# Sliding-window attention on TensorE: token tiles of 128 rows by 32 columns, or of 64 rows by 32 columns with even and odd tokens apart

## The chip, the cores and the metric

The kernel runs on one core of a Trainium2 chip. The metric is the device time of one execution in microseconds (us), the median over several runs. TensorE (PE in the profile, PEld for its weight loads) multiplies matrices and writes its results to PSUM. VectorE (DVE) and ScalarE (ACT) work element by element. SyncE (SP) issues the transfers (DMA) and works through them in order.

## What is computed

x has 2048 tokens of 1024 features, in bf16. Two mixers alternate, each applied twice:

```python
def _A_ref(x, wqkv, wo):              # H = 32 heads, Dh = 32
    W, dil = 8, 2
    qkv = (lambda x, *d: x.transpose(*d))((x @ wqkv).reshape(B, S, 3, H, Dh), 2, 0, 3, 1, 4)
    q, k, v = qkv[0], qkv[1], qkv[2]
    idx = pos[:, None] - (jnp.arange(W) * dil)[None, :]        # 8 keys: token s, s-2, ..., s-14
    ...
    logits = jnp.where(mask, jnp.einsum("bhsd,bhswd->bhsw", q, kg) * scale, -1e9)
    o = jnp.einsum("bhsw,bhswd->bhsd", _softmax(logits, axis=-1), vg)
    return o.transpose(0, 2, 1, 3).reshape(B, S, D) @ wo

def _B_ref(x, w1, b1, w2, b2):        # F = 3584, over the tokens
    u = _gelu(jnp.einsum("bsd,sf->bdf", _layernorm(x), w1) + b1)
    return (jnp.einsum("bdf,fs->bds", u, w2) + b2).transpose(0, 2, 1)

for _ in range(2):
    x = x + _A_ref(_layernorm(x), A_wqkv, A_wo)
    x = x + _B_ref(_layernorm(x), B_w1, B_b1, B_w2, B_b2)
```

A token attends to itself and to seven earlier ones at distances 2, 4, ..., 14: even tokens see only even ones, odd tokens only odd ones.

## The kernel before

The two classes of tokens are called c = 0 and 1. Class c has 1024 tokens, in NI = 8 tiles (c, i) of 128 tokens. Before the change a tile holds tokens of one class only, so that eight neighbours of the window are eight adjacent columns. The 32 heads lie in NG = 8 groups g of four.

One layer runs in stages. The first layer begins with `start_up`: tiles of x are loaded (`x_load`, line 218), normalised on VectorE, transposed into hT by transposing transfers (`T_`, line 281) and multiplied by the value weights (`V_`, line 269); its four queues PE, ACT, DVE and SP are written out by hand, and each engine follows its own list in order. The second layer has hT from the end of `gemm2` and computes the values in `v_proj`.

The attention follows. A unit u is one group of heads and one class; a visit is half a unit, four tiles of 128 tokens, so a layer has 32 visits. In each visit, in this order on TensorE:

- `scores(u, b)` (line 408): keys are the weights, 32 columns at a time; the moving operand is the query qB, which holds each head's query in its own 32 rows and zeros in the others, four heads of 40 columns, 160 in all. ScalarE takes the exponential (line 411) into pc, and `mask` (line 423) on VectorE multiplies by the band into the persistent buffer Pm, in four instructions, one for each 32 partitions.
- `values` of the visit before: value weights of 32 columns against Pm (line 443; line 439 is the overlap from the block before), and the sums of the weights by a matrix of ones (lines 447 and 456). The results lie in the two banks of one PSUM tile, acc, of which there is one buffer. ScalarE makes the reciprocal with a logarithm and an exponential (lines 459, 460), and VectorE multiplies it in (line 462, called norm here), into oT.
- two `qk_chunk`s (line 377): eight matmuls of 512 columns each, the queries or keys of a later unit, in m tiles, of which there are two. ScalarE copies them out (lines 384, 381). The query goes to its rows in qB by VectorE copies (line 388) or by transfers (line 390).

`in_order` keeps TensorE to this written order, and `chain_` keeps another engine to the order in which it is called. In the last two visits of a layer the output projection (`out_proj`, line 492, with its residual add, line 499, and its statistics, line 510) takes the place of the `qk_chunk`s, and there VectorE's order is chained, with the mask in two parts around an add. Then come the rest of the output projection, `gemm1` (line 572) and `gemm2` (line 619), which are dense 128x128 matmuls.

Of the kernel before, what the change touches and what calls it, by code (L numbers as in the profile page):

```python
# [14 lines left out]
P = 128  # L15
# [10 lines left out]
def kernel(  # L26
# [33 lines left out]
    KW = P + W  # L60
    KG = 32
    GW = KG + W
    HB = NI // 2
# [89 lines left out]
    qB = [pers.tile([P, HG, SC + W], BF16, name=f"qB{n}") for n in range(2)]  # L153
    kT = [pers.tile([P, SC], BF16, name=f"kT{n}") for n in range(2)]
    Pm = pers.tile([P, HG, NS * HB, KW], BF16, name="Pm")

    def zero_fill():
        nc.vector.memset(Pm[:].rearrange("p h t k -> p (h t k)"), 0.0)
        for t in qB:
            r = nc.vector.memset(t[:].rearrange("p h t -> p (h t)"), 0.0)  # L160
        return r
# [5 lines left out]
    out_v = out2d.rearrange("(i p c) d -> c i p d", p=P, c=DIL)  # L167
    wq_v = A_wqkv.rearrange("(kt p) c -> p kt c", p=P)
# [32 lines left out]

    last = {}
# [5 lines left out]
    def start_up(v, wv):  # L208
# [3 lines left out]
        def x_load(k, hs=(slice(0, D),)):  # L212
            c, i = order[k]
# [3 lines left out]
            for h in hs:  # L217
                r = nc.sync.dma_start(out=xs[k][:, h], in_=xin_v[c, i][:, h])
# [42 lines left out]
        def C_(k, hf):  # L261
            ks = slice(hf * KD // 2, (hf + 1) * KD // 2)
            return nc.scalar.copy(out=hT[:, ks, cols(*order[k])], in_=tps[k, hf][:])

        def V_(k, n, kts):
            if k not in pss_:
                pss_[k] = a_tile() if k % 3 == 1 else s_tile()
            for kt in kts:
                r = nc.tensor.matmul(pss_[k][:, n, :], lhsT=hT[:, kt, cols(*order[k])], rhs=wv[kt // 2][:, kt % 2, n * 512:(n + 1) * 512],  # L269
# [3 lines left out]
        def E_(k):  # L273
            c, i = order[k]
            dst, src = v[c][i][:].rearrange("p (n d) -> p n d", n=NDC), pss_[k][:]
# [4 lines left out]
        def T_(k):  # L280
            return nc.sync.dma_start_transpose(out=hT[:, :, cols(*order[k])], in_=xs[k])
# [76 lines left out]
    def v_proj(v, c, i, wv, ns):  # L358
        for n in ns:
            ps = m_tile()  # L360
            for kt in range(KD):
                nc.tensor.matmul(ps[:], lhsT=hT[:, kt, cols(c, i)], rhs=wv[kt // 2][:, kt % 2, n * 512:(n + 1) * 512],  # L362
                                 start=(kt == 0), stop=(kt == KD - 1))
            nc.scalar.copy(out=v[c][i][:, n * 512:(n + 1) * 512], in_=ps[:])
# [7 lines left out]
    def qk_chunk(u, wts, part, n):  # L372
        g, c = divmod(u, DIL)
        ps = m_tile()
        lo = c * SC + n * 512
        for kt in range(KD):
            mm = nc.tensor.matmul(ps[:], lhsT=wts[part][:, kt, (g % 2) * P:(g % 2 + 1) * P], rhs=hT[:, kt, lo:lo + 512],  # L377
                                  start=(kt == 0), stop=(kt == KD - 1))
        ls = slice(n * 512, (n + 1) * 512)
        if part:  # L380
            nc.scalar.copy(out=kT[u % 2][:, ls], in_=ps[:])  # L381
        else:
            qs = gop.tile([P, 512], BF16, name="qs", tag="go")
            nc.scalar.copy(out=qs[:], in_=ps[:])  # L384
            for h in range(HG):
                hp = slice(h * DH, (h + 1) * DH)
                if h < 1 + 2 * n or u == 0:
                    nc.vector.tensor_copy(out=qB[u % 2][hp, h, ls], in_=qs[hp, :])  # L388
                else:
                    chain_("SP", lambda: nc.sync.dma_start(out=qB[u % 2][hp, h, ls], in_=qs[hp, :]))  # L390
# [8 lines left out]
    def scores(u, b):  # L399
        q, k = qB[u % 2], kT[u % 2]  # L400
        s0 = (2 * u + b) % NS * HB
        ss = s_tile()
        for i in range(HB):
            lo = (b * HB + i) * P
            for r in range(P // KG):
                rp = slice(r * KG, (r + 1) * KG)
                dst = ss[rp, i // 2, i % 2 * HG * GW:(i % 2 + 1) * HG * GW].rearrange("p (h k) -> p h k", k=GW)
                mm = nc.tensor.matmul(dst, lhsT=k[:, lo + r * KG:lo + (r + 1) * KG],  # L408
                                      rhs=q[:, :, lo + r * KG:lo + r * KG + GW], start=True, stop=True)
        pc = pcp.tile([P, HB, HG, GW], BF16, name="pc", tag="pc")  # L410
        nc.scalar.activation(out=pc[:].rearrange("p (n t) h k -> p n (t h k)", n=2), in_=ss[:, :, 0:2 * HG * GW],  # L411
# [344 lines left out]
```

## Time and profile before

| | |
|---|---|
| time, three runs | 1290.9, 1290.99 and 1291.12 us; median 1290.99 |
| span of the profiled execution | 1288.8 us (its own time is not given; the median is 2.2 us more) |
| TensorE busy | 1273.3 us, 99% of the span |
| VectorE, ScalarE busy | 417.6 us (32%), 368.9 us (29%) |
| granted TensorE clock | 1.000 |
| attention of the first layer, 69.6 to 203 us | TensorE 130.3, VectorE 93.7, ScalarE 89.3 us busy |
| matmuls of lines 408, 443, 447 in all | 29.5 us, 36.9 us, 24.8 us busy |

The span runs from the first to the last instruction. A matmul's duration in the rows holds its way through the array, so neighbouring matmuls overlap in the rows; the distance of their starts tells what each costs. "issue" as a reason for idle time means that nothing which the profile shows was waited for; here it stands where the array changes between tiles of 128x128 and of 128x32. A tile is named in the views by its name in the program.

### The profile page before, as it was taken

How to read it: one execution, taken by the hardware profiler on the slowest of the kernel's cores; microseconds unless marked ns; L12 is line 12 of the kernel's file. 1: busy time of each engine (PE TensorE's matmuls, PEld its weight loads, DVE VectorE, ACT ScalarE, POOL GpSimd, SP SyncE). 2: the span in 40 equal slices, each digit the busy share in tenths (PEclk: the TensorE clock that was granted, in tenths of full speed). 3: DMA queues.
4: the chain of work that ended last, by engine and by line, in shares of the span. 5: the costliest groups of instructions: out<-in, count | busy, mean ns of one | idle time of the engine just before them, and what ended most of it. 6: DMA issues, size and time to landing. Idle time of an engine off the chain costs nothing.

```text
span 1288.8 us, 19376 instructions
## 1 busy us (share of the span) xinstructions
PE 1273.3 (99%) x8266; PEld 591.8 (46%) x8422; DVE 417.6 (32%) x855; ACT 368.9 (29%) x609; POOL 2.4 (0%) x15
## 2 busy tenths in 40 slices
PE   9999999999999999999999999999999999999999
PEld 4444444444444444444444444444444444444444
DVE  7467777820000022322300677688000000111111
ACT  4366664431111110000033666645311111000000
POOL 0000000000000000000000000000000000000000
PEclk9999999999999999999999999999999999999999
DMA  8711124652232244564500111247323222334321
GB/s 239 113 47 50 48 83 134 199 148 73 66 90 68 58 129 121 138 166 124 137 27 1 50 48 51 80 153 222 110 69 94 68 63 83 98 106 138 116 92 33
DMA packets 204103, 126.59 MB, mean 98 GB/s; under 512 B 44273, under 2 KB 183793, under 8 KB 204017
## 3 DMA queue, kind: packets, MB, share of 16 engines
q1 hardware_dynamic: 204016, 125.35, 34.4%
q8 instruction: 66, 1.08, 0.4%
q14 instruction: 21, 0.16, 0.0%
HBM read 96.48 MB, written 16.78 MB: 88 GB/s over the span
## 4 chain that ended last, share of the span: by engine, by line
PE 98%; issue 1%; DMA 0%; DVE 0%; ACT 0%
PE m L377 17%; PE s L619 15%; PE s L572 15%; PE m L492 9%; PE acc L572 7%; PE m L572 7%; PE acc L619 7%; PE m L619 7%; PE m L362 4%; PE s L269 3%; PE s L408 2%; PE acc L269 1%; PE acc L443 1%; PE acc L447 1%; DMA x<-in_A_x_dram 0%
## 5 line engine op out<-in xcount | busy, mean ns | idle before, releaser
L619 PEld LDWEIGHTS <-w 128*128 128x128 bf16 x1820 | 177.0, 98 | 210.2
L572 PEld LDWEIGHTS <-w 128*128 128x128 bf16 x1792 | 175.4, 98 | 211.4
L377 PE MATMUL m<-hT,wqk 128*128 128x512 bf16 x962 | 223.5, 379 | 6.2 <-issue 4.4
L572 PE MATMUL s<-h,w 128*128 128x512 bf16 x878 | 201.3, 379 | 0.8
L619 PE MATMUL s<-g,w 128*128 128x512 bf16 (+1 forms) x912 | 201.0, 374 | 0.7
L621 DVE SCALAR_TENSOR_TENSOR xo<-s,b_sb,xs 128x512 bf16<-128x512 f32 (+1 forms) x33 | 24.4, 739 | 532.9 <-PE s L619 526.6
L377 PEld LDWEIGHTS <-wqk 128*128 128x128 bf16 x1024 | 95.2, 98 | 118.0 <-issue 10.7
L423 DVE TENSOR_TENSOR Pm<-pc,band 32x640 bf16<-32x640 bf16 x256 | 123.6, 483 | 56.2 <-ACT pc L411 49.4
L492 PE MATMUL m<-wo,oT 128*128 128x512 bf16 x500 | 110.6, 379 | 0.8 <-issue 0.3
L572 PE MATMUL acc<-h,w 128*128 128x512 bf16 x440 | 103.1, 379 | 0.5
L619 PE MATMUL acc<-g,w 128*128 128x512 bf16 x436 | 99.7, 379 | 0.5
L572 PE MATMUL m<-h,w 128*128 128x512 bf16 x438 | 98.4, 379 | 0.5
L619 PE MATMUL m<-g,w 128*128 128x512 bf16 (+1 forms) x436 | 96.9, 376 | 0.6
L178 ACT ACTIVATE ln<-mv,eps 128x1 f32<-128x1 f32 x64 | 18.9, 295 | 231.4 <-DVE mv L186 184.8
L492 PEld LDWEIGHTS <-oT 128*128 128x128 bf16 x512 | 49.6, 98 | 60.4 <-issue 1.3
L579 ACT ACTIVATE g<-s,b_sb 128x1024 bf16<-128x1024 f32 x28 | 31.2, 1114 | 158.2 <-PE s L572 146.4
L388 DVE COPY qB<-qs 32x512 bf16<-32x512 bf16 x136 | 38.2, 281 | 95.5 <-ACT qs L384 94.2
L362 PE MATMUL m<-wv,hT 128*128 128x512 bf16 x251 | 55.2, 379 | 0.3
L411 ACT ACTIVATE pc<-s,shift 128x640 bf16<-128x640 f32 x64 | 51.2, 800 | 11.7 <-PE s L408 11.7
L384 ACT CAST qs<-m 128x512 bf16<-128x512 f32 x64 | 37.5, 586 | 48.3 <-PE m L377 47.2
L381 ACT CAST kT<-m 128x512 bf16<-128x512 f32 x64 | 37.5, 586 | 46.4 <-PE m L377 46.4
L499 DVE TENSOR_TENSOR xn<-m,xr 128x512 bf16<-128x512 f32 x64 | 44.2, 691 | 16.9 <-PE m L492 16.4
(67 smaller groups left out, 678.9 us busy)
## 6 DMA issues: line engine op xcount, KB each, us to landing
w<-in_B_w_dram SPq DMA_DIRECT2D x56, 512.0 KB, 3.7
w<-in_B_w_dram SPq DMA_DIRECT2D x64, 448.0 KB, 4.4
wqk<-in_A_wqkv_dram SPq DMA_DIRECT2D x16, 512.0 KB, 5.0
xa<-xn SPq DMA_DIRECT2D x32, 256.0 KB, 2.2
xs<-xa SPq DMA_DIRECT2D x32, 256.0 KB, 3.1
wo<-in_A_wo_dram SPq DMA_DIRECT2D x8, 512.0 KB, 5.3
xr<-in_A_x_dram SPq DMA_DIRECT2D x16, 256.0 KB, 3.3
xb<-xo SPq DMA_DIRECT2D x16, 256.0 KB, 2.6
```

What stands on the lines that cost most here:

```text
L269: r = nc.tensor.matmul(pss_[k][:, n, :], lhsT=hT[:, kt, cols(*order[k])], rhs=wv[kt // 2][:, kt % 2, n * 512:(n + 1) * 512], start=(kt == ...
L362: nc.tensor.matmul(ps[:], lhsT=hT[:, kt, cols(c, i)], rhs=wv[kt // 2][:, kt % 2, n * 512:(n + 1) * 512], start=(kt == 0), stop=(kt == KD - 1))
L377: mm = nc.tensor.matmul(ps[:], lhsT=wts[part][:, kt, (g % 2) * P:(g % 2 + 1) * P], rhs=hT[:, kt, lo:lo + 512], start=(kt == 0), stop=(kt = ...
L381: nc.scalar.copy(out=kT[u % 2][:, ls], in_=ps[:])
L384: nc.scalar.copy(out=qs[:], in_=ps[:])
L388: nc.vector.tensor_copy(out=qB[u % 2][hp, h, ls], in_=qs[hp, :])
L411: nc.scalar.activation(out=pc[:].rearrange("p (n t) h k -> p n (t h k)", n=2), in_=ss[:, :, 0:2 * HG * GW], func=ACT.Exp, scale=scale, bia ...
L423: mm = nc.vector.tensor_tensor(out=Pm[rp, :, s0:s0 + HB, r * KG:r * KG + GW].rearrange("p h t k -> p t h k"), in0=pc[rp], in1=mk, op=ALU.mult)
L492: mm = nc.tensor.matmul(ps[:], lhsT=oT[g][:, cols(c, i)], rhs=wo[n][g // 4][:, g % 4, :], start=(g == 0), stop=(g == NG - 1))
L499: return nc.vector.tensor_tensor(out=xn[:, xs_], in0=pss_["o", n][:], in1=xr[:, xs_], op=ALU.add)
L572: nc.tensor.matmul(pairs[fl][0][dc], lhsT=wt[c][:, i, fl * P:(fl + 1) * P], rhs=h2[c][i][:, dc * 512:(dc + 1) * 512], start=(k == 0), stop ...
L619: nc.tensor.matmul(ap, lhsT=w2t[ft // HF][:, ft % HF, c::DIL], rhs=g[ft // GF][:, ft % GF, lo:lo + w], start=(ft == 0), stop=(ft == FT - 1))
```

## The change

A tile t now holds 128 consecutive tokens, the 64 even ones in rows 0 to 63 and the 64 odd ones in rows 64 to 127. `hT`, `v` and `kT` follow this order; `qB` keeps two slots instead of four, since two heads share 64 rows. A visit is four such tiles of one group of heads (512 tokens, both classes).

- `scores` makes one matmul for 32 keys and two heads (64 rows, 80 columns) where there was one for four heads (128 rows, 160 columns). The head pairs e = 0 and 1 write different PSUM banks.
- `values` makes one matmul for each class (64 rows, 72 columns instead of 136) and likewise for the sums (256 columns instead of 512); class c has PSUM bank c of acc, the values in its first half and the sums in its second.
- the query and key projections run two and three chunks ahead; each query chunk has two VectorE copies and two transfers.
- each tile of x is loaded by two transfers (the first tile by four), and in `gemm2` of the first layer each tile is transposed by two transfers.
- the output projection takes its tiles in another order (four at a time from both classes) and in half tiles: one in visit 29, two each in visits 30 and 31, the others after. VectorE's order is chained in these three visits, with the mask in one piece.

The functions' lines before stand in the listing above; of `qk_chunk`, `scores`, `values` and the visits' loop the lines after are shown.

```diff
-    KW = P + W
     KG = 32
     GW = KG + W
-    HB = NI // 2
+    KH = P // DIL
+    KW = KH + W
+    HB = 4
+    NQ = NT // HB
+    QC = HB * KH
+    NV = NG * NQ
...
-    qB = [pers.tile([P, HG, SC + W], BF16, name=f"qB{n}") for n in range(2)]
-    kT = [pers.tile([P, SC], BF16, name=f"kT{n}") for n in range(2)]
+    qB = [pers.tile([P, 2, DIL, SC + W], BF16, name=f"qB{n}") for n in range(2)]
+    kT = [pers.tile([P, S], BF16, name=f"kT{n}") for n in range(2)]
     Pm = pers.tile([P, HG, NS * HB, KW], BF16, name="Pm")
...
+    xin_m = x_in.rearrange("(t m c) d -> t c m d", m=KH, c=DIL)
...
             if k % 2 == 0:
                 x_load.t = gop.tile([P, GF, D], BF16, name="x0", tag="go")
             xs[k] = x_load.t[:, k % 2, :]
             for h in hs:
-                r = nc.sync.dma_start(out=xs[k][:, h], in_=xin_v[c, i][:, h])
+                for c in range(DIL):
+                    r = nc.sync.dma_start(out=xs[k][half(c), h], in_=xin_m[k, c][:, h])
...
+    def qk_chunk(part, k, wts):
+        g, n = divmod(k, NQ)
         ps = m_tile()
+        lo = n * 512
         for kt in range(KD):
+            mm = nc.tensor.matmul(ps[:], lhsT=wts[g // 2][part][:, kt, (g % 2) * P:(g % 2 + 1) * P],
+                                  rhs=hT[:, kt, lo:lo + 512], start=(kt == 0), stop=(kt == KD - 1))
         if part:
+            nc.scalar.copy(out=kT[g % 2][:, lo:lo + 512], in_=ps[:])
         else:
+            qs = gop.tile([P, DIL, QC], BF16, name="qs", tag="go")
+            nc.scalar.copy(out=qs[:].rearrange("p c (t m) -> p t c m", m=KH),
+                           in_=ps[:].rearrange("p (t c m) -> p t c m", c=DIL, m=KH))
             for h in range(HG):
                 hp = slice(h * DH, (h + 1) * DH)
+                dst = qB[g % 2][hp, h % 2, :, n * QC:(n + 1) * QC]
+                if h % 2 == 0 or k < 2:
+                    nc.vector.tensor_copy(out=dst, in_=qs[hp])
                 else:
+                    chain_("SP", lambda: nc.sync.dma_start(out=dst, in_=qs[hp]))
...
+    def scores(vis):
+        g, b = divmod(vis, NQ)
+        q, k = qB[g % 2], kT[g % 2]
         ss = s_tile()
         for i in range(HB):
+            t = b * HB + i
             for r in range(P // KG):
+                c, f = divmod(r, KH // KG)
                 rp = slice(r * KG, (r + 1) * KG)
+                lo = t * KH + f * KG
+                for e in range(2):
+                    ep = slice(e * 2 * DH, (e + 1) * 2 * DH)
+                    dst = ss[rp, e, i * 2 * GW:(i + 1) * 2 * GW].rearrange("p (h k) -> p h k", k=GW)
+                    mm = nc.tensor.matmul(dst, lhsT=k[ep, t * P + r * KG:t * P + (r + 1) * KG],
+                                          rhs=q[ep, :, c, lo:lo + GW], start=True, stop=True)
         pc = pcp.tile([P, HB, HG, GW], BF16, name="pc", tag="pc")
+        nc.scalar.activation(out=pc[:].rearrange("p t (e h) k -> p e t (h k)", e=2),
+                             in_=ss[:, :, 0:2 * HB * GW].rearrange("p e (t x) -> p e t x", t=HB),
                              func=ACT.Exp, scale=scale, bias=shift[:])
+        exps[:] = pc, vis % NS * HB
...
+            lo = r % (KH // KG) * KG
+            mm = nc.vector.tensor_tensor(out=Pm[rp, :, s0:s0 + HB, lo:lo + GW].rearrange("p h t k -> p t h k"),
...
+    def values(vis, v, oT):
+        g, b = divmod(vis, NQ)
         acc = a_tile()
         t0 = b * HB
+        s0 = vis % NS * HB
         sp = (s0 - 1) % (NS * HB)
+        hc = [(h, c) for h in range(HG) for c in range(DIL)]
         for i in range(-1 if b else 0, HB):
+            for h, c in hc:
+                hp, cp = slice(h * DH, (h + 1) * DH), half(c)
+                lhs = v[t0 + i][cp, g * P + h * DH:g * P + (h + 1) * DH]
                 if i < 0:
+                    dst, src = acc[hp, c, 0:W], Pm[cp, h, sp, KH:KW]
                 else:
+                    w = KW if i < HB - 1 else KH
+                    dst, src = acc[hp, c, i * KH:i * KH + w], Pm[cp, h, s0 + i, 0:w]
+                nc.tensor.matmul(dst, lhsT=lhs, rhs=src, start=(i == (-1 if b else 0)), stop=False, skip_group_check=True)
         runs = [(s0, HB - 1, 1)]
         if b:
             runs = [(sp, HB, 0)] if sp < s0 else [(sp, 1, 0)] + runs
+        for lo_, n_, t_ in [(s0, HB, None)] + runs:
+            for h, c in hc:
+                hp, cp = slice(h * DH, (h + 1) * DH), half(c)
+                dst = acc[hp, c, QC:2 * QC].rearrange("p (t q) -> p t q", q=KH)
+                if t_ is None:
+                    src = Pm[cp, h, lo_:lo_ + n_, 0:KH]
+                else:
+                    dst, src = dst[:, t_:t_ + n_, 0:W], Pm[cp, h, lo_:lo_ + n_, KH:KW]
+                mm = nc.tensor.matmul(dst, lhsT=ones[cp], rhs=src, start=False, stop=t_ is not None, skip_group_check=True)
+        rd = x2("rd", [P, DIL, QC], FP32)
+        nc.scalar.activation(out=rd[:], in_=acc[:, :, QC:2 * QC], func=ACT.Ln)
         nc.scalar.activation(out=rd[:], in_=rd[:], func=ACT.Exp, scale=-1.0)
+        dst = oT[g][:].rearrange("p (c s) -> p c s", c=DIL)[:, :, b * QC:(b + 1) * QC]
+        norm.append(lambda: nc.vector.tensor_tensor(out=dst, in0=acc[:, :, 0:QC], in1=rd[:], op=ALU.mult))
...
-    order = [(c, i) for c in range(DIL) for i in range(NI)]
+    order = [(c, i) for b in range(NQ) for c in range(DIL) for i in (2 * b, 2 * b + 1)]
...
-            nc.sync.dma_start_transpose(out=hT[:, :, cols(c, i)], in_=xs[:])
-
-    NU = NG * DIL
+            for e in range(2):
+                lo = (2 * i + e) * P + c * KH
+                nc.sync.dma_start_transpose(out=hT[:, :, lo:lo + KH], in_=xs[half(e)])
...
+        def half_tile():
+            if not cur:
+                cur.extend(out_proj(*next(tiles), oT, wo, res, xa[li], h2))
+                n = 0
+            else:
+                n = 1
+            in_order(cur[0], n)
+            chain_("DVE", cur[1], n)
+            if n:
+                cur[2]()
+                lns.append(list(cur[3]))
+                cur.clear()
+
+        for part, k in ((0, 0), (0, 1), (1, 0), (0, 2), (1, 1)):
+            in_order(qk_chunk, part, k, wts)
+        for vis in range(NV):
+            ends = vis >= NV - 3
+            if vis % (2 * NQ) == 2 and vis // (2 * NQ) + 1 < NG // 2:
+                nx = vis // (2 * NQ) + 1
+                wts[nx] = [None, None]
+                chain_("SP", load_qk, nx, wts[nx])
+            if vis == NV - 8:
                 wo = []
                 chain_("SP", load_wo, wo)
+            if vis == NV - 3:
                 todo[:] = order
                 for _ in range(3):
                     load_xr(res)
+            in_order(scores, vis)
+            if ends:
+                chain_("DVE", mask, 0, 1, 2, 3)
+            else:
                 mask(0, 1, 2, 3)
             if vis:
+                in_order(values, vis - 1, v, oT)
+                if ends:
+                    chain_("DVE", norm.pop())
+                else:
                     norm.pop()()
+            for part, k in ((0, vis + 3), (1, vis + 2)):
+                if k < NV:
+                    in_order(qk_chunk, part, k, wts)
+                elif ends:
+                    half_tile()
                     ln_step()
+        in_order(values, NV - 1, v, oT)
+        n = 0
+        for n in range(2 * NT - 5):
+            if n in (17, 21):
+                chain_("SP", load_w1, (n - 17) // 4)
+            half_tile()
+            ln_step()
+            if norm:
+                chain_("DVE", norm.pop())
```

## The prediction

> **What bounds the kernel now.** I read the page first: the engines' shares and the chain that ended last.
>
> ```profile
> span 1288.8 us, 19376 instructions
> PE 1273.3 (99%) x8266; PEld 591.8 (46%) x8422; DVE 417.6 (32%) x855; ACT 368.9 (29%) x609; POOL 2.4 (0%) x15
> ...
> PE 98%; issue 1%; DMA 0%; DVE 0%; ACT 0%
> ```
>
> TensorE (PE) is the path nearly everywhere, so only its time counts, and whatever makes it wait. The change touches the attention stages (some 133 us in each layer by the stage windows) and their two ends. So I read TensorE's timeline over two visits (start, duration, engine, line, tile, count):
>
> ```profile
> 117.93 0.46 PE L408 MATMUL s<-qB,kT 128*32 128x160 bf16 x16
> 118.22 0.41 PE L443 MATMUL acc<-Pm,v 128*32 128x136 bf16 x16
> 118.45 0.39 PE L447 MATMUL acc<-Pm,ones 128*32 128x512 bf16 x4
> 118.67 0.18 PE L456 MATMUL acc<-Pm,ones 128*32 128x24 bf16 x4
> 118.78 3.63 PE L377 MATMUL m<-hT,wqk 128*128 128x512 bf16 x15
> 122.34 0.46 PE L408 MATMUL s<-qB,kT 128*32 128x160 bf16 x16
> 122.63 0.18 PE L439 MATMUL acc<-Pm,v 128*32 128x8 bf16 x4
> 122.66 0.40 PE L443 MATMUL acc<-Pm,v 128*32 128x136 bf16 x16
> ...
> 126.78 0.46 PE L408 MATMUL s<-qB,kT 128*32 128x160 bf16 x16
> ```
>
> Read the starts, not the durations, which overlap. A visit takes 4.41 to 4.44 us (122.34 less 117.93, 126.78 less 122.34), of which the 16 projection matmuls take 16 x 0.216 = 3.46 and the attention burst 0.97. In the burst the scores take 0.29, the values 0.23, the sums by ones 0.22 and the rest, with the switch back to full tiles, 0.11. Sixteen score matmuls of 160 columns in 0.29 us are four at a time: 4 x 160 columns at 0.42 ns (216 ns for 512) is 0.27. So the array's columns are the cost, and four column tiles already run together.
>
> **The burst on the array.** The change gives each matmul half the rows, so eight tiles can be in flight. Scores: 32 matmuls of 80 columns, 4 groups of eight; a group of 160 takes 0.069, so one of 80 takes 0.036 and the stage 0.15 instead of 0.29 (with the 0.01 that the first group costs extra). Values: 32 of 72 columns, 4 x 0.032 = 0.13 instead of 0.23. Ones: 8 of 256 columns, 0.11 instead of 0.22. The overlap from the block before (L439) stays one group of 0.03, but is met in three visits of four instead of two: +0.007. Rest and switches as now. Saved: 0.14 + 0.10 + 0.11 - 0.01 = 0.335 us a visit, to about 4.09.
>
> That eight tiles do run together no row shows: bounds are all of it and none. A row for column tiles exists (above), one for row halves does not; I take all of it, since the code gives the two halves different rows and different PSUM banks. "TensorEngine Tiling (Array Packing)", section Available Configurations, of the Trainium skill lists 64x32 as eight tiles that operate independently; no run here shows it yet.
>
> **What comes next when TensorE is faster.** The accumulator has one buffer, so a visit's values wait for the normalisation of the visit before, which VectorE does after the mask. ScalarE, then VectorE, in the same visits:
>
> ```profile
> 122.45 0.59 ACT L381 CAST kT<-m 128x512 bf16<-128x512 f32 x1 [1.14 <-PE m L377]
> 122.93 0.80 ACT L411 ACTIVATE pc<-s,shift 128x640 bf16<-128x640 f32 x1
> ```
>
> ```profile
> 123.76 2.03 DVE L423 TENSOR_TENSOR Pm<-pc,band 32x640 bf16<-32x640 bf16 x4 [1.45 <-ACT pc L411]
> 125.82 0.69 DVE L462 TENSOR_TENSOR oT<-acc,rd 128x512 bf16<-128x512 f32 x1
> ```
>
> Exponential to end of normalisation: 126.51 - 122.93 = 3.58. The exponential follows the cast of the last projection, not the scores, so shorter scores don't move it; it will start 0.30 + 0.14 = 0.44 after the values start. The loop's floor is 0.44 + 3.58 + about 0.06 for the semaphore = 4.08 us. That is the array's 4.09: nothing more can be won, and each 0.05 us that these strided forms take longer costs 3 us in all. The two query copies per visit (0.28 each) fit behind the normalisation. Gain: 62 full visits x 0.335 = 20.8 us.
>
> **The instructions.** A burst was 40 to 48 load-and-matmul pairs; it becomes 80 to 96, about 88, or 176 instructions. Does TensorE's sequencer deliver them? The waits of its queue at line 408, then the weight loads:
>
> ```profile
> L408 PEldq EVENT_SEMAPHORE  x1: 51/51/51, 831.9 to 831.9; - x1
> ```
>
> ```profile
> 832.40 0.26 PEld L408 LDWEIGHTS <-kT 128*32 128x32 bf16 x16 [0.42 <-issue]
> ...
> 832.95 0.32 PEld L456 LDWEIGHTS <-ones 128*32 128x32 bf16 x8
> ```
>
> The wait sits before the burst's first load and was passed at 831.95, 0.45 us ahead. At 832.95, 40 pairs later, the 81st instruction starts, no later than in other visits: at most 1.0 us / 81 = 12.3 ns an instruction. Usually that wait is passed 2.3 to 3 us, some 28 instructions, ahead; so of 176, 148 must come during the burst. From the first score to the last pair the array needs 0.41 us: 2.8 ns an instruction. Each nanosecond above costs 148 x 62 = 9.2 us. The bounds are 0 and 9.2 x 9.5 = 87 us; I take 0, as no burst of the trace shows a late instruction, and keep the far end for the range. "Runtime: NRT & Kernel Launch", section Instruction fetch mechanics, of the skill speaks against the change with an issue floor of about 20 cycles. At a clock of 1.2 GHz ("TensorE: Matmul & The Clock Gate") my estimate from it is 16.7 ns, 128 us more; the 12.3 ns above already contradict it for matmuls.
>
> **The end of attention, twice.** The output projection's half tiles now begin at visit 29, right after values(28), whose first token block is their own input. Seven of eight matmuls cover 1.51 us; the eighth needs norm(28), which VectorE does after mask(29). Counted from the last projection before scores(29): half tile from 0.95, eighth matmul due at 2.46; exponential 0.90 to 1.70, mask to 3.76, norm to 4.48. Stall 2.1 us. At visit 31 values(31) wait again: VectorE has queued two adds (0.69 each), statistics (0.69 each) and mask(31) (2.03) before norm(30), late by some 1.4 us. Today the mask is split between the adds there and no such gap shows. I take 3.5 us a layer, 7 in all (bounds 0, if the order within VectorE hides it, and 10).
>
> **Start-up.** Each x tile is loaded by two transfers instead of one, 17 more issues on SyncE's queue, which also issues the transposes. SyncE, then TensorE:
>
> ```profile
> 20.80 1.25 SPq L281 DMA_TRANSPOSE hT<-x  x1
> 22.09 1.07 SPq L218 DMA_DIRECT2D x<-in_A_x_dram  x2
> 23.25 1.24 SPq L281 DMA_TRANSPOSE hT<-x  x1
> ```
>
> ```profile
> 21.24 3.62 PE L269 MATMUL acc<-wv,hT 128*128 128x512 bf16 x15
> 24.69 7.07 PE L269 MATMUL s<-wv,hT 128*128 128x512 bf16 x32
> ```
>
> An issue takes 0.45 to 0.5 us. The transpose issued at 20.80, with 3.7 us to landing, serves the matmuls at 24.69: slack 0.2. Between it and the transposes before it stand the loads of tiles 7 to 9, three more issues, 1.4 us (the eight extra ones of tiles 0 to 6 lie in front of 14.35, where the queue waits for the first transpose's input today); with the 0.7 by which the first tile is late it slips by 1.5 to 2. The cycle of transpose and two loads then grows from 2.46 to about 3.5, just TensorE's 3.45 a tile, so the slip stays until the loads end. The first tile, four issues instead of two, adds 0.7. I take 2.5 us, bounds 0.7 and 5. The second layer's 16 more transposes (1.24 of issue each) lie beside 12 us of matmul per tile: nothing, and 1.2 us at the last if not.
>
> **Sum.** -20.8 + 7 + 2.5 = -11.3. The profiled span is 1288.8, and about 2.2 us lie around it to the median of 1290.99; that run's own time is not given, so I sum against the median: 1280.
>
> **Rivals.** Slower: the sequencer is the bound. From 2.8 ns an instruction on it decides, at 4.0 the gain is gone, at 6.7 the time is 1280 + 36 = 1316, at 12.3 it is 1367. For it speaks that twice the instructions must pass in half the time and that the trace's bound is loose; against it that 40 pairs pass in 0.8 us without a nanosecond's delay. Second, row halves don't overlap: groups of four at 80, 72 and 256 columns give scores 0.29, values 0.26, ones 0.22 and an overlap of 0.06, +0.06 a visit, with the 9.5 us of the ends 1304. Third, only weight loads of the two halves take turns (a group then costs twice the 0.028 of the 8-column group): scores 0.23, values 0.23, gain 0.16 a visit, 1290: no change.
>
> **How the numbers follow.** This kernel's three runs span 0.2 us and two kernels differ surely by some 0.2%, 2.6 us. Forecast, array or VectorE bound, with up to 3.7 ns: 0.44, its own range 1275 to 1288. Sequencer: 0.40, of which 0.04 within 2.6 us of no change. Halves in turn 0.08. Weight loads in turn 0.05, mostly no change. Ends or start-up worse than their bounds 0.03. So faster 0.44, same 0.08, slower 0.48: the forecast is the likeliest single time, not a safe sign. Below 1275 lies little; cutting the sequencer case at 8 ns leaves about 0.15 above 1328.
>
> **What would show it.** Right: in the timeline visits of about 4.1 us, scores 0.15, values 0.13, ones 0.11, and TensorE waiting on the normalisation by hundredths. Wrong by the sequencer: score groups more than 0.036 apart and idle put down to issue inside the burst, growing behind the first 14 pairs. Wrong by the halves: second halves starting a group's time after the first. The ends show as one idle of 2 us in front of the first output projection, and a shorter one before the last values; start-up as a wait for hT's landing near 25 us.

## The result, and the profile after

The changed kernel takes 1310.49 us (median; 1309.72 to 1312.3), the kernel before 1291.05 beside it: ratio 1.0152, 95% interval 1.0138 to 1.0167. It is slower by 1.5%, where 1280 was forecast. The profiled execution, the slowest of the four, took 1312.3 us with a span of 1310.6, so 21.8 us more than the span before. First the changed kernel's page (span, TensorE's line, the chain):

```profile
span 1310.6 us, 25247 instructions
PE 1285.4 (98%) x11170; PEld 604.9 (46%) x11326; DVE 413.0 (32%) x855; ACT 369.5 (28%) x609; POOL 2.4 (0%) x15
...
PE 93%; DVE 3%; DMA 2%; issue 1%; SPq 1%; ACT 0%; DVEq 0%
```

TensorE is still the path, but the chain now passes through VectorE, transfers and SyncE's queue. By stage (first matmul to first matmul), in us:

| | before | after | difference |
|---|---|---|---|
| start to the first key chunk | 62.68 | 70.34 | +7.65 |
| attention and projection, layer 1 | 197.19 | 204.42 | +7.23 |
| the same, layer 2 | 197.19 | 203.98 | +6.79 |
| gemm1, gemm2, v_proj, each | 193.39, 193.39, 55.25 | 193.39, 193.39, 55.25 | 0 |

A visit of the changed kernel in TensorE's timeline:

```profile
123.58 0.34 PE L423 MATMUL s<-qB,kT 64*32 64x80 bf16 x32
123.82 0.64 PE L460 MATMUL acc<-Pm,v 64*32 64x8 bf16 x40
124.27 0.38 PE L472 MATMUL acc<-Pm,ones 64*32 64x256 bf16 x24
124.58 3.63 PE L387 MATMUL m<-hT,wqk 128*128 128x512 bf16 x15
128.13 0.34 PE L423 MATMUL s<-qB,kT 64*32 64x80 bf16 x32
```

By the starts the scores take 0.24, the values 0.45, the sums with the switch back 0.31; forecast were 0.15, 0.13 and 0.11 with 0.11 behind. A visit takes 4.524 us on average (visits 1 to 24) instead of 4.429. Single records say more. The 32 score matmuls start within 0.139 us, eight in 36 to 41 ns: the row halves do run together. Then nothing starts for 95 ns. From there nearly every matmul starts 8 or 9 ns after the one before, whether it has 72 columns or 8, with further gaps of 34, 95 and 58 ns. The first gap stands behind the 32nd pair of weight load and matmul in every visit from 1 to 31 of both layers (94 to 96 ns), but for visit 26, whose scores wait in the middle: there it stands 32 pairs behind that wait. The 58 ns are the array itself: the eight sums of 256 columns hold it for 256 x 0.42 = 108 ns, and the next matmul on the first one's place starts 117 ns after it.

ScalarE and VectorE keep the pace assumed: from the exponential to the end of the normalisation 3.59 us, forecast 3.58.

```profile
124.17 0.80 ACT L426 ACTIVATE pc<-s,shift 128x640 bf16<-128x640 f32 x1
```

```profile
127.07 0.69 DVE L477 TENSOR_TENSOR oT<-acc,rd 128x512 bf16<-128x512 f32 x1
```

What else TensorE waits for, from its waits (us in total, times, longest):

```profile
PE m L507 <- DVE oT L477: 3.3, 2, 1.6
PE s L423 <- DMA qB<-qs: 2.5, 3, 1.1
PE s L280 <- DMA hT<-x: 2.5, 4, 0.9
PE m L269 <- DVE xc L249: 1.5, 1, 1.5
PE s L280 <- DMA wv<-in_A_wqkv_dram: 1.2, 3, 0.7
PE s L297 <- DVE warm L122: 1.1, 1, 1.1
PE acc L460 <- issue: 0.9, 1, 0.9
PE acc L460 <- DVE oT L477: 0.9, 2, 0.5
```

The first and the last row are the ends of attention that the prediction named, the third to fifth the start-up; the sixth the kernel before has too. The second was not foreseen: scores in visit 26 of each layer. In TensorE's timeline, with SyncE's issues behind it:

```profile
195.93 0.32 PE L423 MATMUL s<-qB,kT 64*32 64x80 bf16 x26
197.23 0.21 PE L423 MATMUL s<-qB,kT 64*32 64x80 bf16 x1 [0.98 <-DMA qB<-qs]
198.55 0.22 PE L423 MATMUL s<-qB,kT 64*32 64x80 bf16 x5 [1.11 <-DMA qB<-qs]
```

```profile
187.25 2.24 SPq L487 DMA_DIRECT2D wo<-in_A_wo_dram  x4
190.47 5.72 SPq L401 DMA_DIRECT2D qB<-qs  x4
```

The last scores of a visit read eight columns of the next query chunk. Its two transfers are issued from 190.47 on, right behind 2 MB of projection weights, and the second lands at 198.5. So the first layer's +7.23 is some 2.7 for the ordinary visits (28 x 0.096), 2.3 in visit 26, 1.63 in visit 29, 0.45 at the last values, and 0.2 left over. In the second layer visit 26 is 1.84 longer, and only part of that is the wait for qB; the rest is the row put to issue, a stop inside the values:

```profile
843.47 0.50 PE L460 MATMUL acc<-Pm,v 64*32 64x8 bf16 x35
844.92 0.21 PE L460 MATMUL acc<-Pm,v 64*32 64x64 bf16 x5 [0.94 <-issue]
```

In SyncE's timeline at start-up the first transposes are issued at 19.53 (14.35 before), and the cycle of a transpose and two loads has gone from 2.45 us to 3.96 (31.48 less 27.52), above TensorE's 3.45 a tile:

```profile
27.52 1.26 SPq L291 DMA_TRANSPOSE hT<-x  x1
28.82 2.56 SPq L229 DMA_DIRECT2D x<-in_A_x_dram  x4
31.48 1.30 SPq L291 DMA_TRANSPOSE hT<-x  x1
```

But more than half of the 7.65 us is lost ahead of that. The value matmuls of the third tile, before and after:

```profile
14.33 7.07 PE L269 MATMUL s<-wv,hT 128*128 128x512 bf16 x32
```

```profile
18.70 3.62 PE L280 MATMUL s<-wv,hT 128*128 128x512 bf16 x16
```

They begin 4.4 us later; the waits for hT, all behind that point, are 2.5 us. From 6 to 14 us the transfer engines are busy throughout in both kernels (share 0.99 and 1.00) but move 280 GB/s instead of 353, so the 64-partition loads seem to be slower to move too, and not only to issue.

### The profile page after: what moved, and what is told of

Its sections match the earlier page's. It is cut to its first block, busy times and chain, and to the rows that moved or that the text cites. A ratio compares the mean times of both kernels' runs of the same rounds, so it can differ in the third digit from the quotient of the medians.

```text
span 1310.6 us, 25247 instructions
## 1 busy us (share of the span) xinstructions
PE 1285.4 (98%) x11170; PEld 604.9 (46%) x11326; DVE 413.0 (32%) x855; ACT 369.5 (28%) x609; POOL 2.4 (0%) x15
## 4 chain that ended last, share of the span: by engine, by line
PE 93%; DVE 3%; DMA 2%; issue 1%; SPq 1%; ACT 0%; DVEq 0%
PE m L387 16%; PE s L634 15%; PE s L587 15%; PE m L587 7%; PE acc L587 7%; PE acc L634 7%; PE m L634 7%; PE m L507 7%; PE m L372 4%; PE acc L460 2%; PE s L280 2%; PE s L423 1%; DMA x<-in_A_x_dram 1%; DMA qB<-qs 1%; DVE Pm L440 1%
## 5 line engine op out<-in xcount | busy, mean ns | idle before, releaser
L387 PE MATMUL m<-hT,wqk 128*128 128x512 bf16 x965 | 228.5, 380 | 3.0
L507 PE MATMUL m<-wo,oT 128*128 128x512 bf16 x496 | 111.4, 379 | 4.1 <-DVE oT L477 3.3
L507 PEld LDWEIGHTS <-oT 128*128 128x128 bf16 x512 | 49.5, 98 | 63.0 <-DVE oT L477 4.3
```

The source lines that it names most:

```text
L387: mm = nc.tensor.matmul(ps[:], lhsT=wts[g // 2][part][:, kt, (g % 2) * P:(g % 2 + 1) * P], rhs=hT[:, kt, lo:lo + 512], start=(kt == 0), st ...
L507: mm = nc.tensor.matmul(ps[:], lhsT=oT[g][:, cols(c, i)], rhs=wo[n][g // 4][:, g % 4, :], start=(g == 0), stop=(g == NG - 1))
```

## Experiments

Theory A: TensorE's instruction supply sets the burst. A queue of 64 instructions (32 pairs of weight load and matmul) fills behind a long chunk; what does not fit comes after a gap, at 8.33 ns a pair. Theory B: the array or its weight loads take those 8.33 ns. The first three runs tell these apart; the others are for the shape of tiles, the start-up and the ends. An ordinary visit is one without a wait; averages are over visits 1 to 24.

**split_burst.** In the changed kernel the key chunk moves between the scores and the values:

```diff
+            work = [(0, vis + 3), (1, vis + 2)]
+            if not ends:
+                in_order(qk_chunk, *work.pop(), wts)
             if vis:
                 in_order(values, vis - 1, v, oT)
...
```

> The changed kernel with one reordering: in each visit the key chunk is issued between the scores and the values, so that the 32 score pairs and the 72 value pairs are two separate bursts, each behind a long chunk of 512-column matmuls. Theory A (TensorE's instruction supply sets the burst: a queue of 64 instructions is filled while a long chunk runs, and what does not fit comes at 8.33 ns per pair of weight load and matmul after a gap of about 95 ns): the values now also start with a full queue, 32 of their pairs go at 3.3 to 4 ns instead of 8.33, and the 95 ns gap ahead of the second value goes; against that stand two more changes between long and short matmuls, about 0.1 us each; net about -0.07 us a visit, 62 visits, so about 1306 us against 1310.5. Theory B (the array or the weight loads take the 8.33 ns whatever the queue holds): nothing is won and the two changes cost 0.2 us a visit, so about 1322 us, and the values stay 8.33 ns apart from the second one on.

Measured: 1318.3 us (ratio 1.0206, 1.0192 to 1.022), between the two. The mechanism is as A has it. The same values burst in TensorE's timeline, cut off at 131.735 and at 131.865:

```profile
131.61 0.32 PE L460 MATMUL acc<-Pm,v 64*32 64x8 bf16 x32
```

```profile
131.61 0.45 PE L460 MATMUL acc<-Pm,v 64*32 64x8 bf16 x39
```

32 values start in the first 0.13 us (3 to 4 ns apart), 7 in the next 0.13: 78 ns of nothing, then 8.33 ns each. The same matmuls in the unsplit kernel come 8.33 ns apart from the second one on. So it is their place behind a full queue that counts. The weight loads are not what takes 8.33 ns: those of the 32 values start 3 to 4 ns apart as well. And while the sums hold the array (no matmul starts between 131.937 and 131.996), the loads behind them keep coming every 8 or 9 ns, so that is the pace at which instructions arrive. The time was mis-sized: ordinary visits fall to 4.48, 0.04 less and not 0.07; visits 4 and 20 of each layer are 0.44 to 0.53 longer; and the wait of visit 26 grows:

```profile
PE s L423 <- DMA qB<-qs: 6.3, 2, 3.6
```

The query chunk is now later, and visits 4 and 20 wait for it too. In visit 4 the 27th and the 28th score start at 98.05 and 98.25, each some 45 ns after one of the query's two transfers landed. These stand on SyncE's queue behind the next weights, as in visit 26:

```profile
97.71 0.75 PE L423 MATMUL s<-qB,kT 64*32 64x80 bf16 x32
```

```profile
90.74 1.21 SPq L379 DMA_DIRECT2D wqk<-in_A_wqkv_dram  x2
93.94 14.44 SPq L401 DMA_DIRECT2D qB<-qs  x7
```

Start-up is 1.4 us longer too, with a granted clock of 0.72 from 6 to 12 us; why it fell there is open. By the profiles, ordinary visits (-2.1), visits 4 and 20 (+1.7), visit 26 (+5.8) and start-up (+1.4) together give the 6.8 us by which its span exceeds the changed kernel's.

**half_values.** Same instructions, half the columns, so that half of the attention's output is left out (the columns of values are 72 and 64, not 80 and 64 as the expectation has it, so 36 and 32 remain):

```diff
-dst, src = acc[hp, c, i * KH:i * KH + w], Pm[cp, h, s0 + i, 0:w]
+dst, src = acc[hp, c, i * KG:i * KG + w // 2], Pm[cp, h, s0 + i, 0:w // 2]
...
-src = Pm[cp, h, lo_:lo_ + n_, 0:KH]
+src = Pm[cp, h, lo_:lo_ + n_, 0:KG]
...
```

> The changed kernel with the same instructions, but the values matmuls and the row-sum matmuls of the 64-column query parts run over half of their columns (40 and 32 for 80 and 64; 128 for 256), and the normalisation reads the written half twice: half of the attention output is left out. Theory A (instruction supply): pairs stay 8.33 ns apart, the visit stays at 4.52 us and the whole at 1310 us within 2. Theory B (columns in the array set the burst): the burst loses about half of what values and row sums take, some 0.11 us of 0.88, so a visit of about 4.41 us and about 1303.5 us.

Measured: 1308.91 us (1.0137, 1.0123 to 1.0151); a visit takes 4.498 us, 0.026 less. In its timeline:

```profile
167.75 0.62 PE L460 MATMUL acc<-Pm,v 64*32 64x8 bf16 x40
168.19 0.31 PE L472 MATMUL acc<-Pm,ones 64*32 64x128 bf16 x16
```

The values still take 0.44 us for 40 pairs, as with twice the columns. What is gone is the gap of 58 ns behind the sums, which with 128 columns hold the array half as long. This is as A has it.

**more_pairs.** The opposite: same columns, 24 pairs more a visit.

```diff
+cuts = [0, KH, KW] if i >= 0 and w == KW else [0, dst.shape[-1]]
+for a, z in zip(cuts, cuts[1:]):
+    nc.tensor.matmul(dst[:, a:z], lhsT=lhs, rhs=src[:, a:z], ...)
```

> The changed kernel with 24 more instruction pairs in a visit's values and the same columns: each values matmul of 72 columns is cut into one of 64 and one of 8. Theory A (instruction supply, 8.33 ns per pair): 24 x 8.33 = 0.20 us more a visit, 62 visits, 12.4 us, so about 1323 us. Theory B (columns in the array, 8 tiles at once): the columns are the same and the short matmuls cost at most what the 8-column groups showed, 28 ns per column tile, so 0 to 0.09 us a visit, 1310 to 1316 us.

Measured: 1323.11 us (1.0247, 1.0232 to 1.0262), 12.6 above the changed kernel; an ordinary visit takes 4.73, 0.21 more, 24 times 8.8 ns. Four of the 48 visits numbered 1 to 24 are 0.36 to 1.03 longer than in the changed kernel, with stops among the sums for which the profile names no releaser; their cause is open.

```profile
136.42 0.86 PE L462 MATMUL acc<-Pm,v 64*32 64x8 bf16 x64
137.09 0.35 PE L474 MATMUL acc<-Pm,ones 64*32 64x256 bf16 x16
```

40 pairs took 0.45, 64 take 0.67. With half_values this settles it: the pairs are paid, not the columns. With split_burst it is their supply, not the array or the weight loads.

**scores_only.** On the kernel before, only the scores in 64-row tiles (`qB` with two slots, the exponential as in the changed kernel):

```diff
+for e in range(2):
+    ep = slice(e * 2 * DH, (e + 1) * 2 * DH)
+    dst = ss[rp, e, i * 2 * GW:(i + 1) * 2 * GW].rearrange("p (h k) -> p h k", k=GW)
+    mm = nc.tensor.matmul(dst, lhsT=k[ep, lo + r * KG:lo + (r + 1) * KG],
+                          rhs=q[ep, :, lo + r * KG:lo + r * KG + GW], start=True, stop=True)
```

> The kernel before with only the scores changed: tiles of 64 rows and 32 columns, two heads at once, 32 matmuls as before, with the other tokens in the rows where they were; values, row sums and start-up stay in the old layout. Theory A (instruction supply): the 32 score pairs are 64 instructions, which fit the queue and run at about 4 ns, and the values at 160 columns need more of the array than their instructions take, so the scores save about 0.15 us a visit, less one gap of up to 0.095 us where the queue has run dry: 0.05 to 0.15 us, so 1282 to 1288 us against 1291. Theory B (a 64-row tile is itself no faster, or the switch costs what it saves): no change, 1291, or slower.

Measured: 1290.8 us, ratio 0.9996 (0.9987 to 1.0005): nothing won; a visit is 0.010 us shorter.

```profile
157.44 0.34 PE L410 MATMUL s<-qB,kT 64*32 64x80 bf16 x32
157.71 0.19 PE L442 MATMUL acc<-Pm,v 128*32 128x8 bf16 x4
```

The 32 scores take 0.139 us as hoped, but the first value comes 0.129 after the last. That can be the supply, as in my expectation, or the step from 64-row to 128-row tiles. The next run tells.

**half_scores.** On the kernel before, two of the four score tiles of a visit in the new form, behind two in the old: `if i < 2:` the old matmul, else the two of scores_only with `q[ep, 2 * e:2 * e + 2, ...]`.

> The kernel before with the scores of only two of a visit's four tiles in 64-row, 32-column form (16 matmuls of 80 columns), behind the other two in the old form (8 matmuls of 160 columns); Exp in two instructions instead of one. It tells apart two readings of the gap of about 0.13 us that followed the 32 score pairs in scores_only. If that gap is the instruction supply starting late (the 32 pairs that the queue held had run out at 0.14 us, and the next instruction came 0.23 to 0.27 us after the burst's start), then here the queue's 32 pairs are 8 old scores, 16 new ones and 8 values, they last about 0.31 us, no gap shows, and the visit loses 0.145 - 0.07 = 0.075 us: about -4.5 us, 1286.5 us. If the gap is the price of going from 64-row to 128-row tiles, it stays, and the kernel takes 1291 to 1294 us.

Measured: 1301.89 us (1.0083, 1.0068 to 1.0098), outside both; a visit takes 4.601, 0.17 more.

```profile
153.28 0.32 PE L409 MATMUL s<-qB,kT 128*32 128x160 bf16 x8
153.53 0.27 PE L415 MATMUL s<-qB,kT 64*32 64x80 bf16 x16
153.73 0.19 PE L449 MATMUL acc<-Pm,v 128*32 128x8 bf16 x4
```

The first 64-row score comes 0.163 us after the last 128-row one, where the next group of the old form comes after 0.070; the first value comes 0.134 after the last score. If the queue holds 32 pairs, 24 of them were still to come at the first gap and 8 at the second, so it had not run dry. So a change of the tile's rows costs 0.09 to 0.12 us by itself (a next group of 64-row scores comes after 0.014 to 0.018), much as the step from a chunk to the burst does (0.309 instead of 0.216). That explains scores_only, and my expectation had counted one such change, not two. In the changed kernel all small tiles have one shape, so there its gap of 95 ns is not this.

**odd_rows_gpsimd.** In the changed kernel:

```diff
-r = nc.sync.dma_start(out=xs[k][half(c), h], in_=xin_m[k, c][:, h])
+eng = nc.sync if c == 0 else nc.gpsimd
+r_ = eng.dma_start(out=xs[k][half(c), h], in_=xin_m[k, c][:, h])
...
```

> The changed kernel with one edit at start-up: the loads of the odd-token half of each input tile are issued from GpSimd's queue, the even half stays on SyncE's. If the extra 7.65 us of start-up come from the number of issues on SyncE's queue (0.63 us each, with the transposes waiting between them), start-up falls by 5 to 7.5 us and the whole to 1303 to 1306 us. If they come from the transfers themselves (64 partitions each, or rows of the input that are taken every second), start-up stays at 62.4 us and the whole at 1310.

Measured: 1310.65 us (1.0147, 1.0132 to 1.0163); first key chunk at 70.32. This looks like the second theory but isn't proof of it. From the transfers view of the first 70 us (count, size, median us to landing):

```profile
x<-in_A_x_dram SPq DMA_DIRECT2D x15, 128.0 KB, 3.7
...
x<-in_A_x_dram POOLq DMA_DIRECT2D x15, 128.0 KB, 7.7
```

What SyncE gained was lost in GpSimd's queue, whose transfers took 4 us longer to land. Inconclusive.

**one_load.** One issue for both halves: `dma_start(out=xs[k][:, h], in_=xin_m[k][:, :, h])`.

> The changed kernel with one edit at start-up: each input tile's even and odd rows are loaded by one issue of 128 partitions (rows taken even first, then odd) instead of two of 64 partitions. If the 7.65 us come with the two issues per tile (their number, 0.63 us each, or their 64 partitions), start-up falls back by 6 to 7.6 us and the whole to about 1303 to 1304.5 us. If taking every second row costs them, start-up stays at 62.4 and the whole at 1310.5 us.

Measured: 1369.94 us (1.0611, 1.0595 to 1.0627); the first key chunk comes at 129.3. A transfer with this source (two classes, then 64 rows, then columns) is itself slow: from 5 to 40 us most slices of its transfers view move 49 to 51 GB/s, where the kernel before reaches 400 with plain transfers, and issues took up to 5 us. The Trainium skill has a reason ("DMA: Bandwidth & Descriptors", section Why a DMA increments its semaphore by 16 and not by 1): a transfer uses the largest number of engines, up to 16, that divides the slowest dimension of source and of destination; in the source here that is the two classes. Two engines of sixteen are an eighth, and this trace agrees: from 25 to 29.9 us the engines' mean busy share is 0.13, and an estimate of 400 / 8 = 50 GB/s fits the rate. The run says nothing on the number of issues.

**two_issues and rows64_before.** On the kernel before, each tile by two issues: of half the columns (`(x_load, k, halves)`), or of 64 partitions (`for a in (slice(0, 64), slice(64, 128))`).

> The kernel before with each input tile loaded by two issues of 128 partitions and half the columns, instead of one issue: the number of issues of the changed kernel, without its 64-partition transfers. If the number of issues on SyncE's queue sets the extra start-up, it grows from 56.35 by 6 to 8 us and the whole is 1297 to 1299 us. If 64-partition transfers are what is slow, start-up stays within 1 us and the whole at 1291 to 1292 us.

> The kernel before with each input tile loaded by two issues of 64 partitions (rows 0 to 63 and 64 to 127 of the same tile) and nothing else changed. In the changed kernel an issue of 64 partitions held SyncE for 0.60 to 0.64 us, in two_issues one of 128 partitions for 0.43. If that price times two per tile is the whole of the extra start-up, the first key chunk comes at 69.5 to 70.5 us instead of 62.68 and the kernel takes 1298 to 1299 us. If the even and odd tokens (rows taken every second, the halves' places) cost something beside it, it stays below 1296 us.

Measured: two_issues 1292.89 us (1.0013, 1.0004 to 1.0022), first key chunk 2.0 later; rows64_before 1297.59 us (1.0049, 1.0035 to 1.0064), just under the 1298 to 1299 of its first theory, with the first key chunk 6.36 later and every later stage as before. SyncE's timeline, two_issues first, then rows64_before:

```profile
26.31 1.24 SPq L281 DMA_TRANSPOSE hT<-x  x1
27.59 2.05 SPq L218 DMA_DIRECT2D x<-in_A_x_dram  x4
29.74 1.39 SPq L281 DMA_TRANSPOSE hT<-x  x1
```

```profile
26.25 1.26 SPq L282 DMA_TRANSPOSE hT<-x  x1
27.56 2.50 SPq L219 DMA_DIRECT2D x<-in_A_x_dram  x4
30.16 1.39 SPq L282 DMA_TRANSPOSE hT<-x  x1
```

Four issues hold SyncE 2.05 us with 128 partitions and 2.50 with 64. The cycles are 3.43 and 3.91 against TensorE's 3.45 a tile: one fits, the other does not. Before it, the first transpose is issued at 14.48 and at 18.33 (14.35 before), and from 6 to 14 us the busy transfer engines move 344 and 314 GB/s (353 before). So 6.4 of the 7.65 us come from the 64-partition loads alone, which are slower to issue and, by this rate, to move; no run takes these two apart. The other 1.3 is no more than start-up differs between runs (69.5 to 71.0 in half_values, more_pairs and wo_and_order, whose start-up is the same).

**pair_loads.** In the changed kernel, from the fifth tile on, one issue for the even rows of two tiles and one for their odd rows:

```diff
...
+if k >= 4:
+    xs[k + 1] = x_load.t[:, 1, :]
+    for c in range(DIL):
+        r = nc.sync.dma_start(out=x_load.t[half(c)], in_=xin_p[k // 2, c])
...
```

> The changed kernel with the input tiles from the fifth on loaded two at a time: one issue for the even rows of two tiles, one for their odd rows, so one issue of 64 partitions per tile instead of two. If issue time on SyncE between the transposes is what the start-up waits for, half of the later issues go, 12 times 0.62 = 7.4 us of SyncE's time; the first four tiles keep their two issues each, so 4 to 6 us come back: about 1305 us. If the rate of the 64-partition transfers sets it, nothing changes: 1310 us.

Measured: 1308.48 us (1.0136, 1.0121 to 1.0152): 2 us back, not 4 to 6. The first transpose comes at 21.1 instead of 19.5, behind the larger transfers, which undoes part of the shorter cycles. Its profile also has a lower granted clock early on: 0.61 from 6 to 12 us and 0.82 from 12 to 18. all_fixes, with the same start-up and a clock of 1.000, has its first key chunk at 68.7, so the clock is not what was missing: the beginning, with its two issues a tile, was left as it is.

**wo_and_order.** In the changed kernel, the projection's weights in four parts, and the last key chunk ahead of the first half tile:

```diff
+            if vis == NV - 3:
+                chunks = chunks[::-1]
...
+            if NV - 10 <= vis < NV - 6:
+                chain_("SP", load_wo, wo, *divmod(vis - (NV - 10), 2))
```

> The changed kernel with two edits of the last visits: the projection's weights are loaded in four parts, one behind the query transfers of each of visits 22 to 25, instead of all at visit 24; and in visit 29 the last key chunk goes ahead of the first half of the projection's first tile. If the wait of the scores in visit 26 (2.35 and 1.84 us) is for query transfers that queue behind 2 MB of weights, it goes, 4.2 us in both layers; if the wait of 1.6 us in visit 29 is for the normalisation of visit 28, the key chunk covers it, 3.3 us in both layers: about 1303 us together. If these waits belong to something else (the instruction supply, or SyncE's issue), they stay at their places or come back at the next visit, and the whole is 1309 to 1311 us.

Measured: 1304.69 us (1.0101, 1.0084 to 1.0117); attention and projection take 200.2 and 200.1 us, 4.2 and 3.9 less. The whole is 5.8 us faster by the medians and 7.4 by the profiled spans, for the 7.5 expected. Its waits, in full from the first row on:

```profile
PE s L280 <- DMA hT<-x: 2.9, 3, 1.5
PE s L280 <- DMA wv<-in_A_wqkv_dram: 2.2, 3, 1.1
PE m L269 <- DVE xc L249: 1.5, 1, 1.5
PE s L297 <- DVE warm L122: 1.1, 1, 1.1
PE acc L460 <- DVE oT L477: 0.6, 2, 0.4
```

The rows of L507 and of qB are gone, and nothing has taken their place. What a layer has left, 3.0 us, is the 28 ordinary visits (2.7).

**all_fixes.** pair_loads and wo_and_order together.

> The changed kernel with pair_loads and wo_and_order together: the terms outside the steady visits taken back as far as they can be. If they are independent: 1304.7 less the 4 to 6 us of pair_loads, about 1299.5 us; what is then left above the kernel before is the steady visits, 2 x 28 x 0.096 = 5.4 us, and some 3 us of start-up. If they hide each other, 1303 us or more.

Measured: 1302.37 us (1.0089, 1.0072 to 1.0106): the two add up (5.8 and 2.0 by their own runs), with pair_loads at its measured size. The best form of the change that was tried stays 0.9% above the kernel before; no version of the changed kernel beat that one.

## Why the prediction was wrong, by its own steps

**The burst on the array: right.** Eight tiles run together. The scores' first-to-last 0.139 us fits the 0.15, and behind a full queue, in split_burst, groups of eight values of 72 columns start 0.032 us apart, as the forecast's 4 x 0.032 has it. The third and the second rival (weight loads or halves in turn) fall with that.

**VectorE's floor: right, and never reached**, as a visit takes 4.52 us and not 4.09.

**The instructions: this step failed.** It had the right count (about 176), the right question and the price that would turn the gain (4.0 ns), and then took 0 because no burst of the trace before showed a late instruction. But no burst there could: a score pair of 160 columns, four tiles at a time, takes the array 0.069 / 4 = 17 ns and a value pair some 15, and 8.33 ns of supply lies hidden under that. The row bounded the supply from above, at 12.3 ns, and nothing bounded it between 2.8 and 12.3. The rate is 4.2 ns an instruction (8.33 a pair), the queue's lead is 64 instructions and not 28, and with the gaps (95, 34 and 95 ns in the visit shown) the burst costs 0.43 us a visit more than forecast: 0.335 not won and 0.096 lost. That is 26 of the 33 us between forecast and result in the profiled spans (30.5 by the medians). This is the first rival, that the sequencer sets the pace, which had been given 0.40. That instructions come too slowly is shown; that it is the sequencer which sets the 4.2 ns, and not something ahead of it, is not. By its own scale the rate alone would give 1280 + 1.4 x 9.2 = 1293 us; the gaps, which it did not have, and the terms below make the rest.

The Trainium skill's floor of about 20 cycles, quoted in the prediction, would be 16.7 ns by the estimate there: matmuls and their loads came four times as fast. Its "TensorE: Matmul & The Clock Gate", section Architectural detail, gives TensorE a queue of 64, and the 32 pairs of split_burst agree; looked up for the lead, it would have replaced the 28.

**The ends: mechanism right, size too large.** Both waits came where they were put: 1.63 us in visit 29 for a forecast of 2.1, and 0.45 at the last values for 1.4. That is 4.2 us in both layers for 7, and wo_and_order takes the first of them away.

**A term was missing.** Visit 26 is 2.3 and 1.84 us longer: the change makes a visit's last scores read into the next query chunk, and so turns a late transfer into a wait. About half of the 1.84 is the stop put to issue, whose cause is open; with the weights' load spread out, in wo_and_order, neither shows. "Every queue that a step is moved past" was not asked of the weights' load, which stayed in its place.

**Start-up: right place, price too small.** 7.65 us for 2.5. An issue was priced at 0.45 to 0.5 by the rows of 128-partition transfers; with 64 partitions it takes 0.60 to 0.64, which puts the cycle at 3.96 instead of 3.5 and so over TensorE's 3.45. And the eight extra issues ahead of the first transpose, taken as hidden, are not: it went from 14.35 to 19.53. two_issues shows that with 128 partitions at 0.43 an issue they would have been. The sum had no term for the loads' lower rate (280 GB/s instead of 353).

By the profiles the terms are: ordinary visits +5.4 for -20.8, ends +4.2 for +7, visit 26 +4.1 for 0, start-up +7.65 for +2.5; together +21.4 of the 21.8. The medians of all runs differ by 19.4, the profiled run having been the slowest of its four.

## What to carry to other kernels

Splitting matmuls into smaller tiles pays in the array only while each pair of weight load and matmul still holds the array longer than the supply takes to bring the next one (here 8.33 ns), or while the whole burst fits the queue (here 32 pairs); and the step to another tile shape inside a burst can eat the gain, as in scores_only. A trace in which the supply never ran short shows only an upper bound of its price: then the cheap test is one run with more pairs at the same columns, ahead of the rewriting. Where a step's data is split in two, price each half's issue and rate by a row of the same shape, count them from the first load on, and compare the cycle with the consumer's 3.45: 3.43 with an undelayed beginning cost 2 us here, 3.91 with a beginning 4 us later cost 6.

## What the runs showed of the hardware that was not expected

- After a long chunk 32 pairs are ready and start 3 to 4 ns apart, as far as the array's columns let them; then come a gap (94 to 96 ns in the changed kernel, 77 to 103 in split_burst's values, but for visit 26) and a pair every 8.33 ns, whatever its columns (8 to 72). What sets the rate, and the later gaps of 34 and some 100 ns, stays open.
- A change of tile shape costs 0.09 to 0.12 us: from 128x128 to 32-column tiles (0.309 instead of 0.216), and in one burst from 128-row to 64-row tiles (0.163 instead of 0.070) and back (0.129 to 0.134 instead of 0.014 to 0.018).
- An issue on SyncE's queue took 0.43 us for 128 partitions and 0.60 for 64 at the same 128 KB; from GpSimd's queue such a transfer landed 7.7 us after its issue, against 3.7. With the transfer engines busy throughout, 64-partition loads moved 280 to 314 GB/s in their mix with the weights, 128-partition ones 344 to 353.
- One transfer that gathers even and odd rows in a single issue fell to some 50 GB/s.
- Behind TensorE's first wait in start-up the mean granted clock from 6 to 12 us was 0.61 in pair_loads (a wait of 1.9 us) and 0.72 in split_burst (2.2), but 1.00 with waits of 1.5 to 1.6 in other profiles, and also with 3.7 in odd_rows_gpsimd. What decides it was not tried.
